# Two tokens per descriptor for the first blocks: a change to a windowed attention and highway kernel

## The chip, the cores and the metric

The kernel runs on one core of a Trainium2 chip. A core has five engines with a queue of instructions each: TensorE (PE, matrix products and transposes), VectorE (DVE), ScalarE (ACT), GpSimd (POOL) and SyncE (SP). They run side by side and wait for one another through semaphores. Sixteen DMA engines move data between main memory and the core's own memory; their work is issued by SP, ACT and POOL. The metric is the device time of one execution in microseconds, as a median of several runs. The time before is 115.41 us, the median of three runs from 115.22 to 116.79.

## What is computed

Four sequences (B) of 768 tokens, eight heads of 64 numbers each. Every query sees the four first keys of its sequence (the sinks) and the 128 keys up to its own position; then a highway layer runs over the 512 numbers of each token:

```python
scores = scale * q @ k.T                       # per batch and head
keep = (pos_k < 4) | ((rel >= 0) & (rel < 128))
a = softmax(where(keep, scores, -1e9))
x = (a @ v)                                    # heads side by side: 3072 x 512
H = maximum(x @ w_h, 0)
T = 1 / (1 + exp(-(x @ w_t + b_t)))
out = T * H + (1 - T) * x                      # float32, 3072 x 512
```

Inputs and output are float32 in main memory; the products run in fp16 with float32 sums.

## The kernel before

The 3072 tokens are cut into 24 blocks of 128, six to a batch; block n belongs to batch n // 6. All work is written as small steps, each for one block, and a single string `_STEPS` (lines 21 to 56) gives their order. The loop at lines 470 to 472 runs through it and emits the instructions of each step. An engine carries out its own instructions strictly in the order of this string, so the string is five queues in one. The planning is thus done beforehand, and nothing is reordered later.

The steps of one block, in the order of the data:

- `lq`, `lk` (`load`, line 140) bring q and k of a block, `[128 tokens, 8 heads, 64]`. For blocks 2 to 23 POOL issues them (line 150), and the DMA casts to fp16. For blocks 0 and 1 SP loads q and ACT loads k in float32 (line 143), and `cvq`, `cvk` (line 168) cast on DVE.
- `lv` (line 146) brings v of one block into `v_all`, for the blocks of batch 0. `lv0`, `lv1` (`load_v`, line 153) bring v of a whole later batch into `v_bat` (`vb` in the profile) in two parts of four heads, all six blocks at once. Every head's 64 columns have a column of ones behind them, so that the product with the weights gives the row sum too.
- `T` (line 258): sixteen transposes on PE of 64 tokens by two heads, out of both partition halves; `cT` (line 272) copies q and k transposed from PSUM to `qk` on ACT, in one instruction of 128x1024.
- `S0`, `S1` (line 304): scores of two head pairs each against the block and its predecessor; `E0`, `E1` (line 320): the exponential on ACT, 128x1024 (128x512 for the first block of a batch); `M0`, `M1` (line 329): the mask on DVE.
- `pks`, `sk`, `es`, `BA`: the sinks. `pks` (line 278) copies sink keys on POOL once per batch, and issues the load of the next batch's sink values; `sv` (line 174) spreads them on DVE. `BA` (line 344) also puts the bias row of the block before into its tile.
- `AV` (line 353): the product with v; `rec` and `x` (lines 375, 380) divide by the row sum on DVE.
- `X`, `cX` (or `cXd` on DVE), `Tt`, `u`, `H`, `d`, `g`, `ee`, `od`: the highway layer. PE transposes x (line 387) and multiplies by both weights (lines 407 and 422, with `lw_t` and `lw_h` loading them); ACT takes a tanh (`u`); DVE does `d`, `g`, `ee` and the last sum in `od` (line 447), whose output SP stores.

Constants: `first` (line 182) sets the ones, the mask and the identity and starts eight matmuls on a zero tile; `pm` and `pb` (lines 194, 202) shape masks on POOL; `K1` copies them; `load_bt` (line 216) loads the bias row twice, on SP, ahead of q; `K2` (line 220) clears the bias rows, sets rows of ones and casts the bias row twice on DVE; `K3` clears `ks_bd`, `K4` (line 233) sets the ones columns of `v_bat` and clears `vs_bd` and `es_t`; `K5` finishes the sink values of batch 0. `_FILL` (line 20) puts idle matmuls ahead of some steps on PE.

Buffers: eight for q and k each, two pairs of PSUM banks for `T` and the scores, one for `AV` and `X` together, two for `Tt`, `H` and `sk`.

Of the kernel before, what the change touches and what calls it, by code (L numbers as in the profile page):

```python
# [8 lines left out]
FP16 = mybir.dt.float16  # L9
# [12 lines left out]
    lk:0 lq:2 lsv:0 K4:0 pm:0 K1:0 cvk:0 lk:1 lbt:0 lq:0 cvq:0 T:0 cT:0 K3:0 S1:0 E1:0 S0:0 E0:0  # L22
    cvk:1 lq:1 cvq:1 T:1 K2:0 lq:3 lv:0 M1:0 cT:1 S1:1 E1:1 S0:1 M0:0 AV:0 lk:2 lk:3 rec:0 x:0 T:3
    E0:1 lv:1 T:2 M1:1 X:0 cT:2 cXd:0 M0:1 S0:2 AV:1 rec:1 x:1 cT:3 S1:3 lw_t:0 lk:4 pb:0 K5:0 pks:0
    E0:2 sv:6 E1:3 M1:3 M0:2 lq:4 S1:2 E1:2 sk:2 es:2 X:1 cX:1 Tt:0 u:0 T:4 cT:4 S0:3 lv:2 M1:2 E0:3
    lw_h:0 BA:2 AV:2 rec:2 x:2 M0:3 Tt:1 u:1 lq:5 g:1 lk:5 g:0 lv:3 X:2 cX:2 S1:4 H:0 d:0 E1:4 M1:4
    H:1 lq:7 T:5 S0:4 d:1 lk:7 ee:1 cT:5 E0:4 BA:3 AV:3 rec:3 lq:6 Tt:2 u:2 sk:4 es:4 x:3 od:1 X:3
    cX:3 S1:5 g:2 ee:0 M0:4 lv:4 E1:5 H:2 S0:5 d:2 E0:5 BA:4 AV:4 od:0 rec:4 lk:6 T:6 lv:5 ee:2 x:4
    cT:6 od:2 lv0:6 Tt:3 M0:5 u:3 X:4 lk:8 cX:4 T:7 cT:7 M1:5 S0:6 H:3 BA:5 AV:5 d:3 g:3 ee:3 lq:8
    E0:6 S1:6 E1:6 rec:5 S0:7 x:5 Tt:4 X:5 od:3 M1:6 E0:7 M0:7 u:4 g:4 T:8 S1:7 lv1:6 cX:5 E1:7 M0:6  # L30
    H:4 Tt:5 lk:9 d:4 lq:9 AV:6 M1:7 cT:8 u:5 ee:4 lk:10 S1:8 E1:8 rec:6 lq:10 x:6 pks:6 H:5 X:6
    od:4 d:5 S0:8 g:5 ee:5 T:9 cX:6 AV:7 rec:7 x:7 lk:11 Tt:6 E0:8 X:7 od:5 cT:9 S1:9 cXd:7 u:6 sk:8
    M0:8 lq:11 lk:13 g:6 E1:9 lk:12 es:8 lq:12 H:6 lq:13 T:10 cT:10 M1:8 d:6 ee:6 S0:9 E0:9 BA:8
    AV:8 rec:8 Tt:7 u:7 T:11 lk:14 cT:11 x:8 X:8 S1:10 od:6 cXd:8 H:7 M0:9 BA:9 E1:10 M1:9 S0:10 d:7
    AV:9 E0:10 rec:9 x:9 g:7 ee:7 M0:10 Tt:8 lq:14 u:8 T:12 X:9 od:7 g:8 cT:12 M1:10 lv0:12 cX:9
    sk:10 es:10 H:8 d:8 S1:11 E1:11 S0:11 E0:11 sv:12 BA:10 AV:10 rec:10 x:10 Tt:9 T:13 ee:8 u:9
    S0:12 E0:12 M1:11 X:10 lv1:12 M0:11 H:9 M0:12 S1:12 cX:10 BA:11 pks:12 lk:15 od:8 AV:11 rec:11
    cT:13 g:9 E1:12 T:14 cT:14 Tt:10 x:11 X:11 cX:11 d:9 ee:9 M1:12 S1:13 S0:13 H:10 od:9 u:10 g:10
    AV:12 rec:12 x:12 E0:13 Tt:11 lq:15 T:15 d:10 M0:13 E1:13 M1:13 lk:18 ee:10 u:11 g:11 X:12 S1:14
    H:11 d:11 cX:12 E1:14 cT:15 AV:13 od:10 S0:14 E0:14 Tt:12 sk:14 u:12 es:14 ee:11 S1:15 E1:15  # L40
    rec:13 lq:17 S0:15 x:13 X:13 od:11 lk:17 lk:16 M0:14 cX:13 M1:14 H:12 d:12 lq:20 T:17 g:12 BA:14
    AV:14 rec:14 x:14 E0:15 lq:16 T:16 M0:15 cT:17 lq:18 ee:12 Tt:13 X:14 lv0:18 M1:15 cT:16 H:13
    cX:14 S1:16 S0:16 u:13 d:13 od:12 E1:16 E0:16 lq:19 BA:15 lv1:18 g:13 AV:15 sk:16 rec:15 ee:13
    S0:17 es:16 E0:17 Tt:14 u:14 x:15 od:13 lk:19 lk:20 S1:17 M0:16 X:15 cX:15 E1:17 H:14 T:18 BA:16
    M1:16 M0:17 AV:16 d:14 Tt:15 cT:18 S0:18 T:19 pks:18 rec:16 g:14 u:15 x:16 X:16 cX:16 E0:18
    ee:14 od:14 H:15 M1:17 BA:17 M0:18 S1:18 g:15 lq:21 d:15 AV:17 rec:17 x:17 Tt:16 lk:21 cT:19
    S1:19 ee:15 E1:18 M1:18 T:20 X:17 cXd:17 u:16 g:16 H:16 od:15 AV:18 cT:20 E1:19 lq:22 rec:18
    x:18 S0:19 d:16 E0:19 M0:19 M1:19 Tt:17 u:17 S1:20 X:18 T:21 cX:18 H:17 cT:21 ee:16 lk:22 AV:19
    d:17 T:22 rec:19 E1:20 x:19 od:16 cT:22 g:17 sk:20 es:20 sv:18 S0:20 ee:17 M1:20 E0:20 M0:20
    X:19 Tt:18 u:18 lq:23 cX:19 od:17 H:18 d:18 S0:21 E0:21 S1:21 E1:21 BA:20 AV:20 rec:20 g:18  # L50
    lk:23 Tt:19 T:23 S1:22 u:19 x:20 M0:21 X:20 cX:20 ee:18 M1:21 cT:23 od:18 g:19 H:19 d:19 BA:21
    AV:21 E1:22 rec:21 S0:22 E0:22 Tt:20 ee:19 x:21 u:20 od:19 M0:22 M1:22 sk:22 S1:23 X:21 cX:21
    S0:23 H:20 es:22 BA:22 AV:22 g:20 d:20 rec:22 x:22 ee:20 E1:23 E0:23 M0:23 Tt:21 u:21 X:22 cX:22
    H:21 M1:23 BA:23 AV:23 d:21 g:21 rec:23 x:23 od:20 Tt:22 u:22 ee:21 g:22 od:21 X:23 cX:23 H:22
    d:22 ee:22 od:22 Tt:23 u:23 g:23 H:23 d:23 ee:23 od:23
# [4 lines left out]
def kernel(  # L60
# [48 lines left out]
    NV = NSC  # L109
# [3 lines left out]
    v_bat = [const.tile([P, VBW + 8], FP16, tag=f"vb{i}", name=f"vb{i}") for i in range(B - 1)]  # L113
# [15 lines left out]
    es_t = [const.tile([P, 2, P], FP16, tag=f"es{i}", name=f"es{i}") for i in range(2)]  # L129
    f32 = {(x, n): const.tile([P, H, D], FP32, tag=f"{x}f{n}", name=f"{x}f{n}")  # L130
           for x, ns in (("q", HWQ), ("k", HWK)) for n in ns}
    f16 = {(x, n): const.tile([P, H, D], FP16, tag=f"{x}h{n}", name=f"{x}h{n}") for x, n in f32}

    sd_of = {}

# [24 lines left out]
    def v_cols(n, h):  # L160
        b, c = divmod(n, NSC)
        if b == 0:
            return v_all[:, n, 65 * h:65 * h + _AVN]
        o = (h * NSC + c) * 65
        return v_bat[b - 1][:, o:o + _AVN]
# [342 lines left out]
```

## Time and profile before

| | value |
|---|---|
| median of three runs | 115.41 us (115.22 to 116.79) |
| the profiled execution | 116.29 us, its span 114.6 us |
| busy: PE, DVE, ACT, POOL | 102.0, 102.2, 91.1, 60.8 us |
| packets in all, under 512 B | 79540, 75426 |
| POOL's DMA queue | 71904 packets, 9.98 MB |
| landing after issue: f32 k, f32 q | 3.9, 5.8 us (medians) |
| landing: q, k on POOL; v by block; v by half batch | 7.3, 7.0; 7.0; 10.8 us |
| issue on POOL: q or k; v by block; half a batch of v | 0.91, 0.90, 1.45 us each |

The profile is of one execution. Its page has the busy time of the engines, the span in forty slices, the DMA queues, the chain of work that ended last, and groups of instructions by source line. Waits are listed as "who <- whom: us in total, times, longest". In the timeline a line gives start, duration, engine, source line, operation, output and inputs, and in brackets the idle time ahead of it with what ended it. Times are in us from the start of the span.

### The profile page before, as it was taken

The page shows a single profiled execution, that of the slowest core. Times are in us where ns is not written, and L with a number is a line of the kernel's source. Part 1 is how long each engine was busy: PE and PEld are TensorE (multiplying, and loading weights), DVE is VectorE, ACT ScalarE, POOL GpSimd, SP SyncE. Part 2 cuts the span into 40 slices and gives each one's busy share as a digit, 9 for nine tenths or more (in the row PEclk, how much of TensorE's full clock was granted, in tenths as well). Part 3 has the DMA queues.
Part 4 walks back from the last instruction along what each step waited for, and adds up shares of the span by engine and source line. Part 5 has one row for each costly group of instructions (what it writes and reads, how often), then busy time and mean ns, then how long its engine had stood idle before and what let it go on. Part 6 is the DMA issues. An engine that isn't in the chain of part 4 may idle for free.

```text
span 114.6 us, 3853 instructions
## 1 busy us (share of the span) xinstructions
PE 102.0 (89%) x1617; PEld 56.4 (49%) x1617; DVE 102.2 (89%) x236; ACT 91.1 (80%) x125; POOL 60.8 (53%) x79
## 2 busy tenths in 40 slices
PE   5956949999999899999999999999998999999910
PEld 2313535555555455556455655646554655644400
DVE  4649569699999999999999999999997999999990
ACT  3137699979999898989989999998898999982500
POOL 5999999796976199704999980003960000000000
PEclk9999999999999999999999999999999999999995
DMA  2999999999999999999999999991899222220332
GB/s 63 244 161 154 198 162 194 156 157 155 156 191 225 181 207 211 215 156 196 166 129 196 194 168 200 212 220 54 112 134 191 36 91 92 96 93 0 123 152 92
DMA packets 79540, 17.56 MB, mean 153 GB/s; under 512 B 75426, under 2 KB 76450, under 8 KB 79524
## 3 DMA queue, kind: packets, MB, share of 16 engines
q0 software_dynamic: 71904, 9.98, 132.0%
q1 hardware_dynamic: 5540, 6.82, 18.4%
q10 hardware_dynamic: 2080, 0.52, 2.0%
q8 instruction: 12, 0.20, 0.7%
q14 instruction: 4, 0.03, 0.1%
HBM read 21.01 MB, written 6.29 MB: 238 GB/s over the span
## 4 chain that ended last, share of the span: by engine, by line
DVE 31%; DMA 24%; PE 19%; POOL 15%; ACT 5%; issue 3%; POOLq 0%; ACTq 0%
DMA ksd<-in_k_dram 14%; DMA vb<-in_v_dram 10%; DVE e L335 8%; PE hps L426 6%; DVE otok L449 6%; DVE xh L382 5%; DVE dd L432 5%; POOL qsd L150 4%; PE av L368 3%; POOL ksd L150 3%; PE tps L414 3%; POOL v_all L146 3%; PE sps L316 3%; DVE gt L438 2%; DVE ee L444 2%
## 5 line engine op out<-in xcount | busy, mean ns | idle before, releaser
L324 ACT ACTIVATE e<-sps 128x1024 f16<-128x1024 f32 (+1 forms) x48 | 44.8, 961 | 2.2 <-PE sps L316 1.9
L274 ACT COPY qk<-tp 128x1024 f16<-128x1024 f16 x24 | 24.3, 1021 | 7.3 <-PE tp L268 7.3
L335 DVE TENSOR_TENSOR e<-e,mask 128x1024 f16<-128x1024 f16 (+1 forms) x48 | 29.2, 638 | 0.2
L426 PE MATMUL hps<-wh_sb,xT 128*128 128x512 f16 x96 | 24.7, 381 | 0.0
L414 PE MATMUL tps<-wt_sb,xT 128*128 128x512 f16 x96 | 24.7, 379 | 0.0
L150 POOL DMA_DIRECT2D ksd<-in_k_dram x22 | 19.9, 910 | 4.5 <-PE av L368 3.1
L150 POOL DMA_DIRECT2D qsd<-in_q_dram x22 | 20.1, 921 | 0.2
L419 ACT ACTIVATE u<-tps 128x512 f16<-128x512 f32 x24 | 14.5, 606 | 5.6 <-PE tps L414 5.4
L316 PE MATMUL sps<-qk 64*128 64x128 f16 x352 | 16.8, 217 | 1.7 <-ACT qk L274 1.7
L382 DVE TENSOR_TENSOR xh<-av,rec 128x512 f16<-128x512 f32 x24 | 16.5, 689 | 0.6
L432 DVE SCALAR_TENSOR_TENSOR dd<-hps,xh 128x512 f16<-128x512 f32 x24 | 16.4, 681 | 0.7 <-PE hps L426 0.7
L449 DVE TENSOR_TENSOR otok<-xh,ee 128x512 f32<-128x512 f16 x24 | 16.4, 683 | 0.1
L368 PEld LDWEIGHTS <-e 128*128 128x128 f16 x352 | 12.8, 97 | 5.5 <-DVE e L335 2.3
L316 PEld LDWEIGHTS <-qk 64*128 64x128 f16 x352 | 10.7, 94 | 8.6 <-issue 6.5
L404 ACT COPY xT<-xtp 128x512 f16<-128x512 f16 x20 | 11.8, 588 | 1.0 <-PE xtp L393 0.7
L368 PE MATMUL av<-vb,e 128*128 128x66 f16 x264 | 11.6, 194 | 0.6 <-DMA vb<-in_v_dram 0.4
L414 PEld LDWEIGHTS <-xT 128*128 128x128 f16 x96 | 8.2, 97 | 7.3
L426 PEld LDWEIGHTS <-xT 128*128 128x128 f16 x96 | 7.7, 98 | 8.0 <-issue 0.3
L285 POOL COPY ks<-qk 64x16 f16<-64x16 f16 x8 | 2.8, 349 | 16.2 <-ACT qk L274 16.0
L444 DVE TENSOR_TENSOR ee<-gt,dd 128x512 f16<-128x512 f16 x24 | 10.0, 417 | 0.3
L156 POOL DMA_DIRECT2D vb<-in_v_dram x6 | 8.7, 1449 | 1.2 <-DMA ksd<-in_k_dram 1.0
L438 DVE TENSOR_SCALAR gt<-u 128x512 f16<-128x512 f16 x24 | 8.6, 363 | 0.0
(66 smaller groups left out, 110.3 us busy)
## 6 DMA issues: line engine op xcount, KB each, us to landing
out_dram<-otok SPq DMA_DIRECT2D x24, 256.0 KB, 5.1
qsd<-in_q_dram POOLq DMA_DIRECT2D x22, 128.0 KB, 7.3
ksd<-in_k_dram POOLq DMA_DIRECT2D x22, 128.0 KB, 7.0
vb<-in_v_dram POOLq DMA_DIRECT2D x6, 384.0 KB, 10.8
v_all<-in_v_dram POOLq DMA_DIRECT2D x6, 128.0 KB, 7.0
kf<-in_k_dram ACTq DMA_DIRECT2D x2, 256.0 KB, 3.9
qf<-in_q_dram SPq DMA_DIRECT2D x2, 256.0 KB, 5.8
wt_sb<-in_moe_w_t_dram POOLq DMA_DIRECT2D x1, 512.0 KB, 6.9
```

The source lines that it names most:

```text
L150: nc.gpsimd.dma_start(out=sd, in_=dram(x, n))
L274: nc.scalar.copy(out=qk.rearrange("p j (a t) -> p a j t", a=2), in_=tp_of.pop(n)[:, :, 0:DM].rearrange("p a (j t) -> p a j t", t=64))
L316: nc.tensor.matmul(sps[:, hh, o:o + P], lhsT=kk[rows, hp, :], rhs=qT[rows, hp, :], start=True, stop=True)
L324: nc.scalar.activation(out=e.rearrange("p a b c d -> p a (b c d)"), in_=sps[:, :, 0:2 * np_ * P], func=AF.Exp, bias=_EXP_BIAS, scale=SCALE)
L335: nc.vector.tensor_tensor(out=ev, in0=ev, in1=m.unsqueeze(1).to_broadcast([P, 4, np_ * P]), op=ALU.mult)
L368: nc.tensor.matmul(av[:, g, 2 * hl + hh, 0:_AVN], lhsT=e[:, hh, hl, pc, :], rhs=v_cols(m, h), start=fresh, stop=False, skip_group_check=True)
L382: nc.vector.tensor_tensor(out=xh.rearrange("p (h d) -> p h d", d=D), in0=av_of.pop(n)[:, :, 0:D], in1=rec_of.pop(n).unsqueeze(2).to_broadc ...
L414: nc.tensor.matmul(t_of[n], lhsT=xT[:, kc, :], rhs=wt_sb[:, kc, :], start=False, stop=(kc == NOC - 1))
L419: nc.scalar.activation(out=uu, in_=t_of.pop(n), func=AF.Tanh, scale=0.5)
L426: nc.tensor.matmul(hps, lhsT=xT[:, kc, :], rhs=wh_sb[:, kc, :], start=(kc == 0), stop=(kc == NOC - 1))
L432: nc.vector.scalar_tensor_tensor(out=dd, in0=h_of.pop(n), scalar=0.0, in1=xh_of[n], op0=ALU.max, op1=ALU.subtract)
L449: nc.vector.tensor_tensor(out=otok, in0=xh_of.pop(n), in1=ee_of.pop(n), op=ALU.add)
```

## The change

Four things are changed together.

1. **q and k of blocks 0 and 1.** Partition p of half a holds the two tokens 2p and 2p+1 of heads 4a to 4a+3, so that each descriptor moves two neighbouring tokens of a head (512 bytes in place of 256). Each load is two DMAs, one per partition half. The cast on DVE sorts the two tokens apart, `T` still makes sixteen transposes, and `cT` puts the tokens back in order in two copies of 128x512.
2. **v of batch 1 by block.** `v_all` holds twelve blocks, `v_bat` two batches; `lv:6` to `lv:11` take the place of `lv0:6` and `lv1:6`.
3. **Constants split.** The two casts of the bias row leave `K2` (DVE) and become `K6` on ACT; the clearing of `vs_bd` and `es_t` leaves `K4` and becomes `K7`, still on DVE.
4. **The order.** `_STEPS` is new from the first to the last line.

```diff
 _STEPS = """
-    lk:0 lq:2 lsv:0 K4:0 pm:0 K1:0 cvk:0 lk:1 lbt:0 lq:0 cvq:0 T:0 cT:0 K3:0 S1:0 E1:0 S0:0 E0:0
-    cvk:1 lq:1 cvq:1 T:1 K2:0 lq:3 lv:0 M1:0 cT:1 S1:1 E1:1 S0:1 M0:0 AV:0 lk:2 lk:3 rec:0 x:0 T:3
-    E0:1 lv:1 T:2 M1:1 X:0 cT:2 cXd:0 M0:1 S0:2 AV:1 rec:1 x:1 cT:3 S1:3 lw_t:0 lk:4 pb:0 K5:0 pks:0
-    E0:2 sv:6 E1:3 M1:3 M0:2 lq:4 S1:2 E1:2 sk:2 es:2 X:1 cX:1 Tt:0 u:0 T:4 cT:4 S0:3 lv:2 M1:2 E0:3
-    lw_h:0 BA:2 AV:2 rec:2 x:2 M0:3 Tt:1 u:1 lq:5 g:1 lk:5 g:0 lv:3 X:2 cX:2 S1:4 H:0 d:0 E1:4 M1:4
...
+    lq:0 lk:0 lq:1 lk:1 lbt:0 pm:0 lk:3 K3:0 lq:3 K4:0 K2:0 cvk:0 K6:0 cvq:0 T:0 cT:0 cvk:1 S1:0
+    E1:0 S0:0 E0:0 cvq:1 T:1 K1:0 M0:0 cT:1 M1:0 K7:0 S1:1 E1:1 M1:1 lk:2 S0:1 E0:1 lsv:0 lv:0 AV:0
+    rec:0 x:0 lq:2 pb:0 T:2 cT:2 T:3 lw_t:0 K5:0 cT:3 pks:0 X:0 cXd:0 S0:2 E0:2 sv:6 sk:2 S1:2 E1:2
+    lv:1 S0:3 es:2 E0:3 M0:1 AV:1 M0:2 Tt:0 lw_h:0 u:0 rec:1 x:1 X:1 cX:1 lq:4 S1:3 E1:3 H:0 BA:2
+    lk:4 T:4 M1:2 g:0 M0:3 lv:2 d:0 ee:0 od:0 Tt:1 AV:2 cT:4 rec:2 S1:4 lk:6 u:1 g:1 S0:4 x:2 H:1
...
-    S0:17 es:16 E0:17 Tt:14 u:14 x:15 od:13 lk:19 lk:20 S1:17 M0:16 X:15 cX:15 E1:17 H:14 T:18 BA:16
-    M1:16 M0:17 AV:16 d:14 Tt:15 cT:18 S0:18 T:19 pks:18 rec:16 g:14 u:15 x:16 X:16 cX:16 E0:18
...
+    lq:19 lk:18 E0:16 Tt:14 u:14 sk:16 lv1:18 x:15 X:15 lv0:18 es:16 lq:20 cX:15 od:11 T:18 ee:13
+    cT:18 M0:16 H:14 S0:17 E0:17 M1:16 BA:16 od:13 g:14 pks:18 lq:21 d:14 lk:21 AV:16 S1:17 E1:17
...
-    H:21 M1:23 BA:23 AV:23 d:21 g:21 rec:23 x:23 od:20 Tt:22 u:22 ee:21 g:22 od:21 X:23 cX:23 H:22
-    d:22 ee:22 od:22 Tt:23 u:23 g:23 H:23 d:23 ee:23 od:23
+    M0:23 ee:20 E1:23 M1:23 Tt:21 u:21 X:22 cX:22 H:21 d:21 g:21 BA:23 AV:23 rec:23 x:23 ee:21 H:22
+    d:22 X:23 cX:23 Tt:22 od:20 u:22 od:21 Tt:23 u:23 g:22 ee:22 od:22 g:23 H:23 d:23 ee:23 od:23
 """
-    NV = NSC
+    NV = 2 * NSC
...
-    f32 = {(x, n): const.tile([P, H, D], FP32, tag=f"{x}f{n}", name=f"{x}f{n}")
+    f32 = {(x, n): const.tile([P, NHP, 2 * D], FP32, tag=f"{x}f{n}", name=f"{x}f{n}")
...
-    f16 = {(x, n): const.tile([P, H, D], FP16, tag=f"{x}h{n}", name=f"{x}h{n}") for x, n in f32}
+    f16 = {(x, n): const.tile([P, 2, NHP, D], FP16, tag=f"{x}h{n}", name=f"{x}h{n}") for x, n in f32}
     def load(x, n):
         if (x, n) in f32:
             eng = nc.sync if x == "q" else nc.scalar
-            eng.dma_start(out=f32[x, n], in_=dram(x, n))
+            b, c = divmod(n, NSC)
+            src = {"q": q, "k": k}[x][b, :, c * P:(c + 1) * P, :]
+            for a in range(2):
+                eng.dma_start(out=f32[x, n][64 * a:64 * a + 64],
+                              in_=src[NHP * a:NHP * a + NHP].rearrange("h (p t) d -> p h (t d)", t=2))
...
     def convert(x, n):
-        nc.vector.tensor_copy(out=f16[x, n], in_=f32[x, n])
+        nc.vector.tensor_copy(out=f16[x, n].rearrange("p t h d -> p h t d"),
+                              in_=f32[x, n].rearrange("p h (t d) -> p h t d", t=2))
...
         for r in (0, 64):
             nc.vector.memset(ones_row[r:r + 1, :], 1.0)
-            nc.vector.tensor_copy(out=bt16[r:r + 1, :], in_=bt32[r:r + 1, :])
+
+    def K6():
+        for r in (0, 64):
+            nc.scalar.copy(out=bt16[r:r + 1, :], in_=bt32[r:r + 1, :])
...
+    def K7():
         for i in range(2):
             nc.vector.memset(vs_bd[i], 0.0)
             nc.vector.memset(es_t[i], 0.0)
...
+        if ("q", n) in f32:
+            for i, sd in enumerate((qsd, ksd)):
+                for j in range(2):
+                    for t in range(2):
+                        for a in range(2):
+                            rows = slice(64 * a, 64 * a + 64)
+                            o = ((i * 2 + j) * 2 + t) * 64
+                            nc.tensor.transpose(tp[:, a, o:o + 64], sd[rows, t, 2 * j:2 * j + 2, :],
+                                                ident[rows, rows])
...
     def cT(n):
         qk = qkT_pool.tile([P, 2 * NHP, P], FP16, tag="qk", name="qk")
-        nc.scalar.copy(out=qk.rearrange("p j (a t) -> p a j t", a=2),
-                       in_=tp_of.pop(n)[:, :, 0:DM].rearrange("p a (j t) -> p a j t", t=64))
+        if ("q", n) in f32:
+            src = tp_of.pop(n)[:, :, 0:DM].rearrange("p a (i j t s) -> p a i j t s", i=2, j=2, t=2)
+            dst = qk.rearrange("p (i a j) (s t) -> p a i j t s", i=2, a=2, t=2)
+            for a in range(2):
+                nc.scalar.copy(out=dst[:, a], in_=src[:, a])
+        else:
+            nc.scalar.copy(out=qk.rearrange("p j (a t) -> p a j t", a=2),
+                           in_=tp_of.pop(n)[:, :, 0:DM].rearrange("p a (j t) -> p a j t", t=64))
```

`v_cols` and `load_v` follow the new sizes of `v_all` and `v_bat`, and `K6` and `K7` are added to the table of steps.

## The prediction

> **What bounds the kernel now.** I read the page first, then the waits, then the timeline of each engine. Parts 1 and 2 of the page give the busy shares and the span in forty slices of 2.9 us:
>
> ```profile
> PE 102.0 (89%) x1617; PEld 56.4 (49%) x1617; DVE 102.2 (89%) x236; ACT 91.1 (80%) x125; POOL 60.8 (53%) x79
> ...
> DVE  4649569699999999999999999999997999999990
> ACT  3137699979999898989989999998898999982500
> ```
>
> The DVE row is read from the left: mixed digits in the first nine slices (26 us), then a wall of nines up to the last slice. DVE is busy 102.2 of 114.6 us. Windows of the same trace put its 12.4 us of idle time at 2.7 us before 6 us, 1.6 us from 6 to 12, 1.1 from 12 to 14, 0.9 from 14 to 18, 1.0 from 20 to 25, and only 2.0 us in all of 25 to 110; 3.2 us lie behind its last instruction. So VectorE is the bound from 25 us on. A change can win in three places only: DVE work taken out, the idle time of the start, and the few late waits. The waits of DVE name them:
>
> ```profile
> DVE rec L377 <- PE av L368: 3.2, 5, 1.2
> DVE qh L168 <- DMA qf<-in_q_dram: 2.2, 2, 1.6
> DVE dd L432 <- PE hps L426: 0.7, 1, 0.7
> ```
>
> Four of the five waits for av lie at 13.04, 16.40, 21.29 and 39.44 us and take 1.17, 0.89, 0.82 and 0.16 us; the wait for hps is at 88.65. ScalarE's timeline shows what paces the start:
>
> ```profile
> 7.50 1.01 ACT L274 COPY qk<-tp 128x1024 f16<-128x1024 f16 x1 [4.33 <-PE tp L268]
> 8.90 1.09 ACT L324 ACTIVATE e<-sps 128x512 f16<-128x512 f32 x2 [0.38 <-PE sps L316]
> 10.30 1.01 ACT L274 COPY qk<-tp 128x1024 f16<-128x1024 f16 x1 [0.32 <-PE tp L268]
> 11.80 1.94 ACT L324 ACTIVATE e<-sps 128x1024 f16<-128x1024 f32 x2 [0.49 <-PE sps L316]
> 14.30 1.93 ACT L274 COPY qk<-tp 128x1024 f16<-128x1024 f16 x2 [0.56 <-PE tp L268]
> ```
>
> From its first copy at 7.50 ScalarE runs with gaps of half a microsecond, each copy of block 0 and 1 releasing scores, and the scores an exponential. The start of cT:0 is the term to follow.
>
> **The loads of blocks 0 and 1.** Now each moves 1024 runs of 256 B; afterwards 512 runs of 512 B, in two issues. The ACT queue (q10) carried 2080 packets in 2.0% of 16 engines' 114.6 us: 36.7 us, or 17.6 ns a packet. In the window of 60 to 90 us the output queue took 20.0% of 480 us for 1151 packets of 2 KB, 83 ns each. A straight line between the two gives about 27 ns for 512 B (my estimate). The four tiles then cost 2048 x 27 / 16 = 3.5 us against 4096 x 17.6 / 16 = 4.5: 1.0 us less. The last of them, q of block 1, lands at 1.94 + 6.5 = 8.45 now, that of block 0 at 6.57. With q0 and k0 first on both queues (data flows from 2.0 us at 209 to 253 GB/s) 524 KB are in at about 4.5, and cvq:0 (0.43) ends at 5.0. T:0 doesn't start then: PE's fill matmuls in front of it run from 4.65 to 6.15. T:0 goes from 7.05 to about 6.2 and could release cT:0 at 6.6, 0.9 us before today.
>
> The Trainium skill, page "DMA: Bandwidth & Descriptors", speaks on both sides. Its section Specifications gives 512 B as the smallest transfer at full rate, which agrees with the direction of the two rows above. Its section "Rules for kernel authors" says not to bother splitting a transfer over two partition halves, since both halves run on the same engines one behind the other; no run here shows that yet. By that rule the halves win nothing over one issue and only the run length counts; the sum above already takes nothing for the halves.
>
> **K6, the bias casts on ScalarE.** Two casts of 1x512 leave DVE (1.16 us) and go to ACT between cvk:0 and T:0, thus ahead of cT:0 in ACT's queue. The trace has no such row on ACT; 128x512 forms take 0.59 (copy) and 0.61 (tanh), so the pair costs between 0 and 1.2 us; I take 1.1. They wait for bt32, and its two DMAs, now first on SP at 0.81 and 1.22, are issued last, behind four issues of 0.41 to 0.72 us. The second is then issued between 3.0 and 4.3 and, with the 2.0 us that the quickest DMA of the trace takes to land, can be there at 5.0 at the earliest. On SP's queue the tiles land in the order of issue (6.57, 8.45), so I expect bt behind q1. Now the f32 tiles need 6.45 us from 2.0 on, 4.5 of their own and 1.9 shared with the POOL loads; afterwards 3.5 and, as the first POOL load moves behind the mask selects (1.7 to about 2.3), some 1.2 shared: 6.7. The ends are 5.0 and 8.45; I take 6.7, nearest to the row of q1 less the saved microsecond. K6 ends at 7.8 and cT:0 starts there, against 7.50. Queued behind K6 on ACT are cT:0, E1:0, E0:0, cT:1, and for cT:0 wait S1:0, pks:0 and with it POOL's next loads.
>
> **cT in two halves.** 128x512 copies take 0.59 each: 1.18 for 1.01, the strided write unknown; between -0.1 and +0.4 each, taken as +0.15, for two blocks +0.3. The same 16 transposes are issued in T. **Start: cT:0 from 7.8 to 8.95 instead of 8.51, and 0.15 more in block 1: +0.6** (bounds -0.65 and +2.4).
>
> **The DVE edits.** K4 loses one buffer's two memsets (0.16), v_all's two memsets double (0.09 more at most). K7 (1.3 us) moves from 2.6 us to behind M1:0. K2's casts now end at 11.08 and hold M0:0 back from 9.99 to 11.11; but DVE waits for av right after, so their going is worth nothing there: 13.04 is set by AV:0. The permuted casts of q and k write runs of 64 elements; 0.36 to 0.54 us now, at most doubled, beside idle DVE time. If that cover went, 0.4 us in block 0.
>
> **The order from 13 to 25 us.** Afterwards M1:1 can start at about 13.4 (E1:1's end plus the shift). DVE's queue then reads rec, x, K5, cXd, sv, M0:1, M0:2, rec, x, M1:2. Eleven instructions at their row times, less the 0.07 us by which neighbours overlap, are 6.0 us: M1:2 ends at 19.4 without a wait, if lv:1 (issued about 10.1, landing 5.7 to 9.0 later in the v_all row) is in for AV:1 at 17.2. Today M1:2 ends at 20.47 with one more mask (0.6) in it: 0.5 ahead. Then M0:3, g:0, d:0, ee:0 and od:0 (2.4 us) stand in front of rec:2, where today 0.82 us are idle; H:0 and Tt:1 ahead of AV:2 on PE take 2 us, so about half of that wait returns. I take **-0.6**, the ends being -1.9 (all idle time gone) and +0.8 (one more wait of the size of 0.82).
>
> **v of batch 1 by block.** POOL pays 6 x 0.90 for 2 x 1.45, +2.5 us. What hides it: POOL waits 16.0 us at pks. The six are issued one by one and AV:6 no longer needs both halves of vb, which now hold it at 39.1:
>
> ```profile
> PE av L368 <- DMA vb<-in_v_dram: 0.4, 1, 0.4
> POOL ks L285 <- ACT qk L274: 16.0, 2, 10.9
> PE tp L268 <- DMA ksd<-in_k_dram: 0.6, 1, 0.6
> ```
>
> DVE idles 0.16 us there: **-0.2** (0 to -0.2). If the cover goes, lv:6 comes late for AV:6; by issue times of 0.9 it goes out near 27 and lands near 35, some 3 us early.
>
> **T:21.** The third line above is at 87.35: k of block 21 is issued at 80.49, because POOL stood at pks:18 until cT:18 ended at 78.95. DVE idles 0.71 us at 88.65 for it. In the new order cT:18 stands ahead of E0:17 and E1:17 on ACT (two times 1.03), and PE has H:14, S0:17 and S1:17 more between T:18 and T:21. The load is early by more than the 0.6 it lacked; next late on PE is only its own work. **-0.6** (0 to -0.7).
>
> **Tail.** From x:23 on DVE has the same eleven instructions; now 0.26 us lie in a gap at 106.6 that od:20 and od:21 would fill: **-0.15** (+0.3 to -0.3).
>
> **Sum:** 0.6 - 0.6 - 0.2 - 0.6 - 0.15 = -0.95. The profiled execution took 116.29 (span 114.6 and 1.7 around it), 0.9 above the median of 115.41: 115.3 for such an execution, 114.5 as a median.
>
> **Rivals.**
> 1. *The bias row comes last and ScalarE stands in front of it.* For it: SP's two tiles landed in order, and 8.45 for q1 is measured while 512 B is an estimate. Against it: fewer packets. If bt lands at 8.45, K6 ends at 9.55 and cT:0 at 10.7: +2.35 for the start, -1.55 from the rest: 116.2, slower. It decides from a landing of 7.65 on (K6 to 8.75, cT:0 to 9.9). If AV:1 or AV:2 waits too (+0.8 for -0.6), 117.6. By the page's rule on halves the loads win least, and this is the case that it favours. Chance 0.24.
> 2. *The bias row is early*, since it is a few packets that needn't wait for all engines. At 5.0 K6 is over by 6.1, T:0 sets cT:0 at 6.6: start -0.65 + 0.15 and, the exponentials coming half a microsecond earlier, up to -1.5 in the second stage: 115.41 - 0.5 - 1.5 - 0.95 = 112.5. Chance 0.22.
> 3. *The order gives nothing*: waits move, DVE stays full after 25 us, and T:21's wait comes back at another block: 115.41 + 0.6 - 0.2 - 0.15 = 115.7, no change. Chance 0.14.
>
> The forecast has 0.40. The range 112.2 to 117.2 takes in rivals 2 and 1 and leaves out both worst ends (111.5 and 118.4). Two per cent, which is about what a measurement of this kernel can tell, is 113.1 and 117.7. Faster by more: rival 2 and a little of the forecast, 0.24; slower by more: the worse part of rival 1, 0.10; within: 0.66.
>
> **What would show it.** The first cast on ACT (1x512) starts near 6.7 and waits for DMA bt; T:0 near 6.2; the first copy of block 0 at 7.8 in two rows of 0.59. DVE has no wait of 0.9 for av between 14 and 18, none at 39 and none for hps near 88; its busy time is 1.2 us lower. The prediction is wrong if bt lands after 7.65 or before 5.5, if AV:1 waits for v_all, or if a wait of over half a microsecond appears on DVE behind 25 us.

## The result and the profile after

The changed kernel takes **120.86 us** (median of four runs, 120.29 to 121.43) against 115.67 for the kernel before in the same comparison (115.22 to 116.79): a ratio of **1.042, with an interval of 1.035 to 1.048**. It is slower; the forecast was 114.5, and the whole range ended at 117.2. An execution can be disturbed (the kernel before itself ran from 115.1 to 119.2 on the chips used below), and ratios are formed from the undisturbed ones alone, so that a ratio and two medians need not agree to the last half per cent.

The profiled execution took 121.43 us with a span of 119.7, 5.1 more than the 114.6 of before. Parts 1 and 2 of the page of the kernel after (busy time; then forty slices of 3.0 us):

```profile
PE 104.8 (88%) x1617; PEld 57.6 (48%) x1617; DVE 102.4 (86%) x232; ACT 92.7 (77%) x129; POOL 62.3 (52%) x83
...
DVE  5354065889999999999999999999999999999980
ACT  0007858999999788998898999999989999893500
...
PEclk9997555999999999999999999999999999999999
```

DVE is busy as long as before (102.4 for 102.2 us), although two casts have left it. Its wall of nines begins in the tenth slice (27 us) and has no gap up to the tail; before, it began in the ninth (23 us) and had a 7 at 86 to 89 us. ACT does nothing at all in the first three slices. And the clock granted to TensorE falls to half in slices 5 to 7, where the row of before has no low digit but the last:

```profile
PEclk9999999999999999999999999999999999999995
```

What ACT was waiting for stands in its timeline (start, duration, line, operation, idle time ahead of it and what ended it):

```profile
0.81 2.70 ACTq L146 DMA_DIRECT2D kf<-in_k_dram  x4
9.68 1.28 ACT L235 ACT_TABLE_LOAD   x1 [9.68 <-DMA bt<-in_moe_b_t_dram]
10.98 1.24 ACT L235 CAST bt<-bt 1x512 f16<-1x512 f32 x2
12.23 1.32 ACT L299 COPY qk<-tp 128x512 f16<-128x512 f16 x2
14.04 1.08 ACT L351 ACTIVATE e<-sps 128x512 f16<-128x512 f32 x2 [0.49 <-PE sps L343]
15.86 1.32 ACT L299 COPY qk<-tp 128x512 f16<-128x512 f16 x2 [0.73 <-PE tp L280]
```

The wait for the bias row ends at 9.68. Only then does ACT load its function table, then it casts the bias row twice, and cT:0 starts at 12.23 instead of 7.50. Before, the table load waited for nothing and was over by 3.2 us:

```profile
1.89 1.28 ACT L274 ACT_TABLE_LOAD   x1 [1.89 <-issue]
```

The transposes that cT:0 copies had been ready since 8.1.

The waits of DVE in the kernel after (who, for whom, us in total, times, longest):

```profile
DVE e L362 <- ACT e L351: 6.0, 3, 4.1
DVE kh L172 <- DMA kf<-in_k_dram: 3.2, 2, 1.7
DVE warm L188 <- PEq L517: 0.9, 1, 0.9
DVE rec L404 <- PE av L395: 0.7, 2, 0.4
```

The waits for av have shrunk from 3.2 to 0.7 us, and the one for hps is gone. In their place the first masks wait 6.0 us for the first exponentials.

**Two halves of the story.** Let the first reciprocal (rec:0) divide the span. It starts at 13.04 before and at 19.94 after: the start has lost 6.9 us. From rec:0 to the last reciprocal (rec:23) it was 92.0 us and is now 90.0: everything behind the start has won 2.0. The tail behind rec:23 is 9.7 for 9.55. 6.9 - 2.0 + 0.2 is the 5.1 us of the span. Windows from rec:0 to rec:23 show where the 2.0 come from (length, then busy time of PE, PEld, DVE, ACT, POOL). Before:

```profile
13.04:105.05 92.01, 88.24 (x1508) 50.85 (x1507) 88.16 (x188) 83.80 (x116) 49.12 (x57) 1.00 1.67 157
```

After:

```profile
19.94:109.97 90.03, 88.44 (x1508) 51.25 (x1507) 87.85 (x187) 83.12 (x116) 48.74 (x58) 1.00 1.68 153
```

DVE's idle time between the two marks goes from 3.85 us (92.01 - 88.16) to 2.18: 1.67 us less. The rest is DVE's own durations, 0.3 us.

**The 6.9 us of the start** add up from single rows: cT:0 starts 4.73 later, is 0.31 longer (two copies of 0.66 for one of 1.01), and from its end to rec:0 it takes 6.39 us instead of 4.53, 1.86 more. This last part has the low clock in it. The windows of after that hold it (columns as above, the eighth number is the clock):

```profile
9.00:11.00 2.00, 0.00 (x0) 0.00 (x0) 1.30 (x6) 1.30 (x2) 0.00 (x0) 0.81 3.14 141
11.00:14.00 3.00, 0.40 (x8) 0.34 (x8) 0.06 (x1) 2.52 (x4) 0.33 (x3) 0.50 1.60 193
14.00:18.00 4.00, 3.50 (x33) 1.41 (x30) 2.03 (x6) 2.53 (x5) 4.00 (x7) 0.50 0.80 54
18.00:21.00 3.00, 2.97 (x37) 1.54 (x35) 1.71 (x6) 2.44 (x3) 3.00 (x4) 0.58 1.17 162
```

PE runs out of work at 8.8 and waits for the copy cT:0 until 13.6. A mean of 0.81 in the window of 9 to 11 puts the drop near 10.2, and 0.58 in that of 18 to 21 the return near 20.5. In between eight score products take 0.61 us where they took 0.40.

### The profile page after: what moved, and what is told of

Same layout as the page of the kernel before. It is cut to its first block, busy times and chain, and to the rows that moved or that the text cites. A ratio compares the mean times of both kernels' runs of the same rounds, so it can differ in the third digit from the quotient of the medians.

```text
span 119.7 us, 3869 instructions
## 1 busy us (share of the span) xinstructions
PE 104.8 (88%) x1617; PEld 57.6 (48%) x1617; DVE 102.4 (86%) x232; ACT 92.7 (77%) x129; POOL 62.3 (52%) x83
## 4 chain that ended last, share of the span: by engine, by line
PE 57%; DVE 27%; DMA 7%; ACT 5%; issue 1%; ACTq 0%
PE hps L453 13%; PE tps L441 11%; PE sps L343 9%; PE av L395 8%; DVE e L362 5%; DMA bt<-in_moe_b_t_dram 5%; DVE otok L476 5%; DVE dd L459 5%; DVE xh L409 5%; PE tp L289 4%; DVE ee L471 3%; DVE gt L465 3%; DMA kf<-in_k_dram 3%; PE sk L323 2%; PE xtp L420 2%; PE sps L258 2%
## 5 line engine op out<-in xcount | busy, mean ns | idle before, releaser
L301 ACT COPY qk<-tp 128x1024 f16<-128x1024 f16 x22 | 22.1, 1020 | 0.8 <-PE tp L289 0.7
L343 PE MATMUL sps<-qk 64*128 64x128 f16 x352 | 17.5, 224 | 4.8 <-ACT qk L299 4.8
L409 DVE TENSOR_TENSOR xh<-av,rec 128x512 f16<-128x512 f32 x24 | 16.5, 688 | 0.6
L476 DVE TENSOR_TENSOR otok<-xh,ee 128x512 f32<-128x512 f16 x24 | 16.3, 685 | 0.2
L459 DVE SCALAR_TENSOR_TENSOR dd<-hps,xh 128x512 f16<-128x512 f32 x24 | 16.3, 680 | 0.0
L312 POOL COPY ks<-qk 64x16 f16<-64x16 f16 x8 | 2.3, 285 | 22.7 <-ACT qk L301 17.5
L150 POOL DMA_DIRECT2D v_all<-in_v_dram x12 | 10.9, 908 | 1.7 <-DMA wh_sb<-in_moe_w_h_dram 1.3
L235 ACT ACT_TABLE_LOAD x1 | 1.3, 1283 | 9.7 <-DMA bt<-in_moe_b_t_dram 9.7
```

Source lines behind the costliest of these rows:

```text
L301: nc.scalar.copy(out=qk.rearrange("p j (a t) -> p a j t", a=2), in_=tp_of.pop(n)[:, :, 0:DM].rearrange("p a (j t) -> p a j t", t=64))
L343: nc.tensor.matmul(sps[:, hh, o:o + P], lhsT=kk[rows, hp, :], rhs=qT[rows, hp, :], start=True, stop=True)
L409: nc.vector.tensor_tensor(out=xh.rearrange("p (h d) -> p h d", d=D), in0=av_of.pop(n)[:, :, 0:D], in1=rec_of.pop(n).unsqueeze(2).to_broadc ...
L459: nc.vector.scalar_tensor_tensor(out=dd, in0=h_of.pop(n), scalar=0.0, in1=xh_of[n], op0=ALU.max, op1=ALU.subtract)
L476: nc.vector.tensor_tensor(out=otok, in0=xh_of.pop(n), in1=ee_of.pop(n), op=ALU.add)
```

## The experiments

The theory from these profiles was: *the bias row comes last on SP's queue, and everything on ACT stands behind it*. Rivals were that the new loads themselves are late, that the halved clock is the price, that the table load behind the wait is, and that the new order is worse. Each kernel below is the one named, with one edit. cT:0 and rec:0 are start times from the profile of the run; the ratio is to the kernel before on the same chip, with its interval of 95%.

**1. Bias row first, all else as after (e1_bt_first).**

```diff
-    lq:0 lk:0 lq:1 lk:1 lbt:0 pm:0 lk:3 ...
+    lbt:0 lq:0 lk:0 lq:1 lk:1 pm:0 lk:3 ...
```

> The changed kernel with the bias row's load first on SP instead of last. Theory A (ScalarE's queue stands behind the bias row: it landed at 9.68 us, then came the table load of 1.28, the casts of 1.24 and only then cT:0 at 12.23): cT:0 starts at the end of T:0, near 8.3, TensorE's clock doesn't drop at 10 us, and the time falls by 4.0 to 4.8 us to about 116.4. Theory C (the new order or the loads are what is slow): cT:0 starts early all the same, but the time falls by less than 2 us, to 119 or more.

Measured: 117.49 us, ratio 1.011 (1.006 to 1.016). Some 3% of the 4.2% are gone, so the place of the bias row on the queue carries most of the loss. But the kernel is still not faster than before, and against the expectation the clock fell here too (from 9.6 to 16.4 us). ACT's timeline in this run:

```profile
3.88 1.28 ACT L239 ACT_TABLE_LOAD   x1 [3.88 <-issue]
5.18 1.25 ACT L239 CAST bt<-bt 1x512 f16<-1x512 f32 x2
7.74 1.32 ACT L303 COPY qk<-tp 128x512 f16<-128x512 f16 x2 [1.32 <-PE tp L284]
...
12.71 1.32 ACT L303 COPY qk<-tp 128x512 f16<-128x512 f16 x2 [2.18 <-PE tp L284]
```

cT:0 is back where it was (7.74), cT:1 isn't (12.71 for 10.30): q of block 1 is cast at 11.53 only, and DVE waits 2.3 us for it. With the bias row last (after) the same cast ran at 9.96, and with the old loads and the row first (5, below) at 8.21: in these profiles q is late with the new loads, and later still with the row's two issues ahead of it.

**2. More idle matmuls while PE waits (e2_fill).**

```diff
-_FILL = {'T:0': 4, 'S1:0': 3, ...
+_FILL = {'T:0': 4, 'S1:0': 25, ...
```

> The changed kernel with 25 idle matmuls ahead of S1:0 instead of 3, so that TensorE works from 8.0 to about 13.4 us, where it stood idle. Theory B (the halved clock from 10 to 21 us is a cost of its own): granted clock 1.0 throughout, S1:0 still at 13.6, and 1.0 to 2.0 us less: about 119.3. Theory A alone (only the late start counts, ScalarE paces the stretch anyway): within 0.4 us of the changed kernel, 120.5 to 121.

Measured: 121.02 us, ratio 1.032 (1.025 to 1.039). Inconclusive. In its profile the clock held until about 16.3 and then fell all the same, and the bias row, issued 0.7 us later, landed at 10.67, a microsecond later than in the profile of after. From the end of cT:0 to rec:0 it took 5.7 us for 6.4. The interval overlaps that of after.

**3. The table load ahead of the wait (e3_table).** An 8-element copy on ACT, of a tile that DVE has cleared, is put behind the two k loads; it has no part in the output.

```diff
-    lq:0 lk:0 lq:1 lk:1 lbt:0 ...
+    lq:0 lk:0 lq:1 lk:1 tb:0 lbt:0 ...
+        "tb": lambda n: nc.scalar.copy(out=tb_b, in_=tb_a),
```

> The changed kernel with a copy of 8 elements on ScalarE behind its loads of k, so that the table load comes there and not behind the wait for the bias row. Theory A: the table load is done by 6 us, the casts start at 9.7, cT:0 at 10.95 instead of 12.23, and the time falls by 1.3 us, and a little more for a shorter time at the halved clock: 119.2. If the late start is caught up later by idle time of VectorE: less than 0.4 us.

Measured: 119.94 us, ratio 1.023 (1.018 to 1.029), thus 1.8% below after. ACT in this run:

```profile
3.55 1.28 ACT L494 ACT_TABLE_LOAD   x1 [3.55 <-issue]
```

The table is now loaded at 3.55, and the casts start at 10.69 without it. That this is the landing of the bias row is inferred: the profile lists the wait under a mask instruction of DVE that ended just then, with which the casts have nothing to do. So the table load did stand on the path. It is 1.28 us long, 1.1% of the time; the 1.8% measured are more than that, within the intervals. The profile doesn't show the whole of it at the start: with the row a microsecond later, cT:0 is only 0.3 us earlier than in after and rec:0 0.35, and 1.15 us of its shorter span lie between rec:0 and rec:23, in shorter DVE instructions.

**4. The new loads alone (e4_loads).** The kernel before, with the loads, casts, `T` and `cT` of the change and its own order, constants and v.

> The kernel before with the new loads, casts, T and cT of blocks 0 and 1 alone; order, bias casts and v as before. Theory A, with the loads as measured in the changed kernel (an issue of a half takes 0.64 to 0.86 us against 0.41 to 0.72 for a whole tile, a 512-byte packet 35 ns against 17.6 for 256): no gain, cT:0 later by 0.3 to 1.0 and each cT by 0.3, 116.0 to 117.0. As I predicted the loads (27 ns a packet): cT:0 half a microsecond earlier, 115.0 to 115.6.

Measured: 118.52 us, ratio 1.012 (1.006 to 1.018). cT:0 at 8.54 and cT:1 at 12.17, against 7.50 and 10.30. The loads alone lose; the clock was at half from 7.5 to 14.3, and how much of the loss that makes isn't separated.

**5. All but the new loads, bias row first (e5_bt_first_old_loads).** After, with `lbt:0` first as in 1 and `load`, `convert`, `T`, `cT` of before.

> The changed kernel with the bias row's load first on SP and the old loads, casts, T and cT for blocks 0 and 1: what is left of the change is the new order, v of batch 1 by block and the casts on ScalarE. Theory A (the bias row's place and the loads make up the whole loss; with the bias row first 1.1% of it is left, and the loads alone cost 1.15%): cT:0 starts by 7.6 us, the clock holds, ratio to the kernel before 0.990 to 1.003. Theory C (the new order costs something of its own): ratio above 1.006.

Measured: 114.25 us, ratio **0.978 (0.967 to 0.989): faster than before**. ACT in this run:

```profile
2.19 1.28 ACT L234 ACT_TABLE_LOAD   x1 [2.19 <-DMA bt<-in_moe_b_t_dram]
3.48 1.25 ACT L234 CAST bt<-bt 1x512 f16<-1x512 f32 x2
8.11 1.01 ACT L283 COPY qk<-tp 128x1024 f16<-128x1024 f16 x1 [3.37 <-PE tp L277]
```

The wait for the bias row is still on the table load, but the row is there at 2.19, 1.4 us after its issue at 0.81, and all of it is over 3.4 us before cT:0 can start. The gain was more than expected, although cT:0 starts at 8.11 and not by 7.6 and the clock fell (from 9.8 to 13.3). What is left of the change, the order with v by block and the split constants, gains: 88.7 us from rec:0 to rec:23 where it was 92.0. Of these 3.3 us, 1.7 are less idle time of DVE, as forecast; the other 1.6 are shorter instructions on DVE, which nobody forecast (1.2 of them in the `g` steps, of which more in the last section).

**6. All but the new loads, bias row still last (e6_old_loads).** After, with the four functions of before; the bias row now stands behind two issues on SP instead of four.

> The changed kernel with the old loads, casts, T and cT alone; the bias row stays last on SP, behind two issues instead of four. Theory A1 (the bias row lands behind whatever stands on SP's queue; q of block 1 landed at 8.45 in the kernel before): it lands at 8.0 to 9.0, the table load and the casts end 2.5 us later, cT:0 starts near 11.0, ratio 1.025 to 1.035. Theory A2 (it was the four slow issues that made the bias row late; issued at 2.0 it lands by 5.5): cT:0 before 8.2, ratio below 1.01.

Measured: 117.80 us, ratio 1.013 (1.008 to 1.018); cT:0 at 9.96, between what the theories gave. The difference to 5, on the same chip, is the place of the bias row alone: 3.5%. The row was issued at 1.92 here and is waited for until 7.38:

```profile
7.38 1.28 ACT L230 ACT_TABLE_LOAD   x1 [7.38 <-DMA bt<-in_moe_b_t_dram]
```

That is 5.5 us after issue behind two loads; in after it is 5.7 us behind four (3.93 to 9.68), in 5 it is 1.4 behind none. The time is not made of so much per issue ahead: in these profiles the 2 KB row lands about when the loads ahead of it do.

**7 and 8. What in the loads is late: the two issues, or the longer runs?** One kernel splits the load of before over partition halves and keeps its runs of 256 B (e7_halves); the other has runs of 512 B in one issue over 64 partitions (e8_one_issue). Both start from the kernel before.

```diff
-            eng.dma_start(out=f32[x, n], in_=dram(x, n))
+            for a in range(2):
+                eng.dma_start(out=f32[x, n][64 * a:64 * a + 64], in_=dram(x, n)[64 * a:64 * a + 64])
```

```diff
-            eng.dma_start(out=f32[x, n], in_=dram(x, n))
+            eng.dma_start(out=f32[x, n], in_=src.rearrange("h (p t) d -> p h (t d)", t=2))
```

In the second, the first diff being e7's, all eight heads lie on partitions 0 to 63, `T` reads both head halves from there, and `convert` and `cT` are those of the change.

> The kernel before with the f32 loads of blocks 0 and 1 issued as two partition halves each, runs of 256 bytes as before. If the second issue is what makes the new loads slow (0.64 to 0.86 us for each half): q of block 0 lands after 7.0, cT:0 starts at 8.0 to 8.7, the clock drops at about 8 us, ratio 1.006 to 1.015, as with the new loads alone. If it is the runs of 512 bytes (35 ns a packet, no gain per byte): landings as in the kernel before (6.6 and 8.5), ratio 1.000 to 1.004. By the rule of the Trainium skill (page DMA: Bandwidth & Descriptors, section Rules for kernel authors) that halves go one behind the other on the same engines, the data itself takes as long as before, and only the issues are added.

> The kernel before with runs of 512 bytes in a single issue: two tokens of all eight heads on 64 partitions, transposes out of those 64, cT in two copies. The casts take 64 partitions x 1024 elements, about 0.9 us each instead of 0.45. If the second issue is the slow part: a tile's issue takes 0.4 to 0.7 us and q of block 0 lands by 6.2, earlier than before. If 512-byte packets are no faster per byte: it lands at 6.6 or later. The time of the whole is not the point here, since casts and cT are longer: 115.7 to 118.

Measured: e7 120.73 us (118.88 to 121.61), ratio 1.027 (1.012 to 1.041), more than expected; e8 118.10 us, ratio 1.016 (1.005 to 1.026). Both lose, each in its own way. The loads of q in the two kernels (issue on SP, durations in ns least/median/most, first and last start; then the time to landing). Kernel e7:

```profile
L144 SPq DMA_DIRECT2D qf<-in_q_dram x4: 596/632/694, 1.5 to 4.3; - x4
...
DMA to landing us min/median/max: 4.8/6.0/6.6
```

Kernel e8:

```profile
L145 SPq DMA_DIRECT2D qf<-in_q_dram x2: 625/652/679, 1.5 to 2.2; - x2
...
DMA to landing us min/median/max: 5.0/6.8/8.5
```

Half a tile takes as long to issue as a whole one (0.60 to 0.69 us; the two whole tiles of before took 0.41 and 0.72), so two halves cost twice the issue time, and the last is issued at 4.3 instead of 1.9; q of block 1 is cast at 12.55 instead of 8.50. In one issue of 512-byte runs this is avoided, but then the landing itself takes 8.5 us for q of block 1 where it took 6.5. Fewer packets were no cheaper there: queue q10 of e8 carried 1056 packets in 2.4% of 16 engines' span, 42 ns each, against 17.6 for half the bytes before. (In e8 the casts on 64 partitions are longer too, 0.69 to 1.00 us, and `cT` has two halves; both are part of its loss. Whether the longer runs or the 64 partitions make its landing late isn't separated.)

**9. The clock, with the good version (e9_clock).** Kernel 5, with idle matmuls that leave PE no gap ahead of T:0.

```diff
-_FILL = {'T:0': 4, 'S1:0': 3, 'T:1': 1, ...
+_FILL = {'T:0': 9, 'S1:0': 4, 'S0:0': 1, 'T:1': 1, ...
```

> The kernel with the bias row first and the old loads, with more idle matmuls: nine ahead of T:0 (four before), four ahead of S1:0 (three), one ahead of S0:0, so that TensorE has no gap of 1.1 us ahead of T:0. Theory B (the halved clock is a cost of its own): the clock stays at 1.0 where it fell to 0.5 from 9.9 to 13.3 us, S1:1 and S0:1 end about 0.8 us earlier, ratio to the kernel before 0.966 to 0.974. Theory A alone (ScalarE and the landings pace this stretch): 0.976 to 0.982, as without them.

Measured: 113.98 us, ratio 0.986 (0.977 to 0.994). The window of 9 to 11 us shows the clock held (5 has 0.71 there, and 0.62 from 11 to 14):

```profile
9.00:11.00 2.00, 1.71 (x28) 0.82 (x28) 0.54 (x4) 1.35 (x3) 1.66 (x4) 1.00 2.74 150
```

From the end of cT:0 to rec:0 it is 4.96 us for 5.79 in 5: 0.8 us on the path of the start. In the total it can't be told from 5; the intervals overlap, and the ratio lies above what either theory gave.

**10. v of batch 1 back in two parts (e10_v_halves).** Kernel 5, with `v_all` and `v_bat` of before, and the two parts `lv0:6` and `lv1:6` in place of `lv:6` to `lv:11`; `lv:5` changes places with the first part, since block 5 needs it sooner.

```diff
-    ... lv:7 T:7 BA:4 AV:4 E0:5 lv:5 ...   lv:6 lq:11   lv:8 ... lv:11
+    ... lv:5 T:7 BA:4 AV:4 E0:5 lv0:6 ...  lv1:6 lq:11
```

> The kernel with the bias row first and the old loads, with v of batch 1 in two parts of four heads again. My prediction gave v by block 0.2 us: ratio 0.976 to 0.984. If POOL's shorter issue (2 x 1.45 for 6 x 0.90 us) counts more: below 0.976; if AV:6 comes to wait for the second half: 0.985 to 0.995, with a wait of AV for vb of over half a microsecond near 35 us.

Measured: 117.02 us, ratio 1.004 (0.998 to 1.011), where kernel 9 on the same chip has 0.986: 1.9% of 115.4, or 2.2 us, and more than any of the three cases expected. AV:6 waits for the second part of v, and DVE for AV:6. The lines of PE and of DVE:

```profile
40.38 0.28 PE L377 MATMUL av<-vb,e 128*128 128x66 f16 x4 [2.37 <-DMA vb<-in_v_dram]
```

```profile
40.70 0.21 DVE L386 RECIPROCAL rec<-av 128x8 f32<-128x8 f32 x1 [2.35 <-PE av L377]
```

(The profiled execution took 117.85 us, its quickest 115.86; the place of the wait is from the profile, the price from the ratio.) Without v by block the new order is worth nothing that can be measured.

**11. The bias casts on DVE again (e11_casts_dve).** Kernel 5, with K6 on DVE.

```diff
-            nc.scalar.copy(out=bt16[r:r + 1, :], ...
+            nc.vector.tensor_copy(out=bt16[r:r + 1, :], ...
```

> The kernel with the bias row first and the old loads, with the two casts of the bias row on VectorE at the same place in the order (behind the cast of k of block 0, where VectorE waits for q). If their move to ScalarE is worth nothing with the bias row there, as I predicted for the place of the casts: ratio 0.974 to 0.983. If ScalarE was relieved or VectorE is short of time there: 0.984 to 0.990.

Measured: 113.94 us, ratio 0.984 (0.976 to 0.992), as kernel 9 on the same chip. Moving the two casts off DVE neither gains nor costs once the row is there in time. (Kernel 9 has its fills as a second difference; 14 below differs from 9 by the casts alone and has 0.985 for 0.986, on another chip.)

**12. The casts later on ACT, the rest as after (e12_casts_later).** The bias row stays last on SP; only K6 moves behind E0:1.

```diff
-    ... cvk:0 K6:0 cvq:0 T:0 cT:0 ... S0:1 E0:1 lsv:0
+    ... cvk:0 cvq:0 T:0 cT:0 ...      S0:1 E0:1 K6:0 lsv:0
```

> The changed kernel with its new loads and the bias row last on SP, the two casts on ScalarE moved behind E0:1. Theory A (it is the place in ScalarE's queue that costs, not the late bias row itself): the table load is over by 5.5 us, cT:0 starts at T:0's end near 8, ratio 1.008 to 1.022, as with the bias row first (1.011) and up to 1.2 us for casts in a busy stretch. If it isn't the queue: 1.03 or more.

Measured: 117.65 us, ratio 1.017 (1.009 to 1.025). ACT in this run:

```profile
3.82 1.28 ACT L303 ACT_TABLE_LOAD   x1 [3.82 <-issue]
8.44 1.32 ACT L303 COPY qk<-tp 128x512 f16<-128x512 f16 x2 [3.34 <-PE tp L284]
```

With the same loads and the bias row as late on the queue, cT:0 starts at 8.44 and not at 12.23; the casts run at 16.64 without a wait. So a late row costs nothing by itself; the place of its casts in ACT's queue did. The ratio is close to that of 1, and what remains above kernel 5 is put down to the loads, with a clock at half from 9.7 to 16.5.

**13. v by block alone, in the old order (e13_v_alone).** The kernel before, with twelve blocks in `v_all`, `lv:6` and `lv:7` at the places of the two parts and `lv:8` to `lv:11` behind the q loads of blocks 9 to 12.

> The kernel before with v of batch 1 by block alone, its loads put where the halves stood and behind q of blocks 9 to 12. If the late stall is worth what it shows in the kernel before (0.16 us of VectorE at 39.4 us): ratio 0.995 to 1.003. If v by block is worth two per cent by itself, as in the new order: 0.975 to 0.985. In the first case the wait for vb is only as short as it is because the old order reaches AV:6 late, and two parts of the change are worth something only together.

Measured: 117.65 us as a median of four, its quickest 115.48 where the kernel before had 115.11 on the same chip; no ratio could be formed. No wait for v is left at AV:6, and the stretch from rec:0 to rec:23 is 91.8 us with 4.1 of DVE idle, against 92.0 with 3.9: its profile shows no gain. What v by block is worth in the old order stays open.

**14 and 15. Casts on DVE with and without the fills (e14_casts_dve_clock, e15_casts_dve_again).** Kernel 11 with the fills of 9, and kernel 11 once more.

> New order, v by block, bias row first, old loads, casts of the bias row on VectorE, and the added idle matmuls ahead of T:0, S1:0 and S0:0. Theory B: the clock stays at 1.0, the path from cT:0 to rec:0 is 0.5 to 0.9 us shorter than without them, and the time is 0.3 to 0.8 us below that of the kernel without them. Theory A alone: no difference between the two.

> The same kernel without the added idle matmuls: the clock falls to half for some 3 us behind 9 us. Ratio to the kernel before 0.978 to 0.988 by either theory; it is the other half of the comparison.

Measured: 113.78 us, ratio 0.985 (0.980 to 0.991), and 113.84 us, 0.984 (0.979 to 0.990). The same. But in the profile of the second the clock held too (mean 0.988 over the span), so the pair doesn't price the clock. In both it is 4.95 us from the end of cT:0 to rec:0, as in 9. Kernels 11 and 15 do price it, for they are one program: in the profile of 11 the clock was at half from 9.8 to 13.2, and this way took 5.66 us, 0.7 more.

**The parts together.** Order, v by block and split constants with the bias row first: -2.2% in kernel 5, -1.5 to -1.6% in 9, 11, 14 and 15. The new loads on top: +3.3% against 5 (1), 2.6% against the other four; 12, where the bias row is out of the way in another manner, says +3.2% against those four. The bias row last instead of first: +3.0% with the new loads (after against 1), +3.5% with the old ones (6 against 5). So two parts of about 3% each stand against one of about 2%. In the old order the loads took 1.2% (4); why they cost more in the new one was not settled. In the profile of every kernel with the new loads the clock was at half for 6.8 us or longer at the start (3.4 in 2), so what a late landing costs and what the clock costs are one sum here. The best versions, 5, 9, 11, 14 and 15, take 113.8 to 114.3 us, 1.5 to 2.2% less than the kernel before.

## Why the prediction was wrong

**What bounds the kernel: right.** From rec:0 on DVE is the bound in both kernels (idle 3.85 of 92 and 2.18 of 90 us), and a lost start is not made up behind it.

**The loads: this step failed first.** It took 27 ns for a packet of 512 B, on a straight line between two rows, and from it that the tiles land a microsecond earlier. The sum counted packets and left out the issues. In the changed kernel each half takes 0.62 to 0.86 us to issue. The loads of q in after:

```profile
L146 SPq DMA_DIRECT2D qf<-in_q_dram x4: 624/669/860, 0.8 to 3.2; - x4
...
DMA to landing us min/median/max: 5.2/5.7/6.7
```

And in the kernel before:

```profile
L143 SPq DMA_DIRECT2D qf<-in_q_dram x2: 413/566/718, 1.5 to 1.9; - x2
...
DMA to landing us min/median/max: 5.1/5.8/6.5
```

For q nothing has changed from issue to landing (medians 5.7 and 5.8), though each issue brings half as much. The last issue is 1.3 us later (3.2 for 1.9), and q of block 1 is cast at 9.96 instead of 8.5: later by just about that. For k the last issue is 1.6 us later (2.9 for 1.3) and the way to landing longer too (median 4.9 for 3.9, longest 6.2 for 4.7): by these figures k of block 0 landed at 5.8 for 4.0, and k of block 1 at 9.1 for 6.0. T:0 started at 7.66, not at 6.2. Of this, 0.8 us are longer casts of block 0, 0.90 and 0.76; the writing in runs of 64 isn't the reason, since in kernel 1 the same casts took 0.43 each. The packet itself had no one price: 27.5 ns in e4, 35 in after, 42 in e8 (q10's share of the span over its packets), for 17.6 with half the bytes. At its best that is a fifth less per byte, at its worst a fifth more.

The prediction weighed two sections of the Trainium skill, page "DMA: Bandwidth & Descriptors". Section Specifications has 512 B as the smallest transfer at full rate; here runs of 512 B came in no sooner than runs of 256 B (q of block 0 is cast at 6.58 in e8 and at 6.57 in the kernel before). Its "Rules for kernel authors" say not to split a transfer over partition halves; e7 agrees (1.027), and shows as a reason what the section doesn't name, the second issue.

**K6: right in its mechanism, far too small in size.** The prediction put the bias row "behind q1", and it did land close to q of block 1 (9.68, cast of q1 at 9.96). What was wrong was when that is: 6.7 was taken and 8.45 named as the latest, since q1 was thought to come earlier than today, never later. That is 3.0 us. The second miss, 1.3 us, was in no term: the table load stands ahead of the first activation on ACT, and by moving casts that wait for a DMA to the head of ACT's queue the change put the wait ahead of the table load as well. In before the load ran at 1.89 beside the DMAs, and had no part in the sum. The casts took 1.24 for 1.1. 3.0 + 1.3 + 0.1 is the way from the predicted 7.8 to 12.23.

The Trainium skill, page "ScalarE: Activation LUTs", section "What ACT_TABLE_LOAD costs", gives 1283 ns for the load itself; the 1.28 us in all the timelines above agree. No run here shows the drain that it adds for a switch from one set to another.

**Rival 1** (bias row last, ScalarE in front) named this cause; kernels 1, 6 and 12 show it. The landing from which it was to decide, 7.65, was too late: in kernel 6 the row landed at 7.38, and its place still cost 3.5%, since the table load comes on top. Its price was wrong by 4.7 us (116.2 for 120.86): it took 8.45 for the landing, left the table load out, and gave the gain of the other steps in full against a delay of 2.35 that was really 6.9 at rec:0.

**What follows cT:0.** The start was taken to shift as a whole, with 0.15 us more for block 1's copy. Instead the way from cT:0 to rec:0 grew by 1.86 us. By single profiles: 0.43 are in the new order itself (4.96 in e9 with the old loads and a full clock, against 4.53 before), 0.83 in a clock halved for 3.4 us (5.79 in 5 against 4.96 in 9), 0.40 more where it is halved for nearly the whole way (6.19 in 6, still with the old loads), and the last 0.20 (6.39 in after) come with the new loads, whose cT:1 is 0.31 longer. So the halved clock, which was a rival, is some 1.2 of the 6.9 us of the start. The prediction read the clock row as full and didn't ask what keeps it so.

**cT in two halves:** 0.31 more per block, in the bounds (0.15 taken).

**Order, v by block, T:21: right.** Predicted -0.6, -0.2 and -0.6, together -1.4. Measured: 1.67 us less idle time on DVE from rec:0 to rec:23, of it 0.83 up to rec:7 (predicted 0.8 for order and v) and 0.84 behind it (0.6 for T:21). It isn't a gift of the late start, which gives the loads more time: kernel 5, with rec:0 at 14.91, has 1.72 less. No wait stands at AV:6 or T:21. **The tail** won nothing (0.15 predicted): from rec:23 to the end of the last DVE instruction it is 6.44 us in both. One size in it was misread: v by block was priced by the 0.16 us that DVE waited in the old order, but in the new one, which needs v sooner, the two parts would have cost 2.2 us (10). Whether it is a gain by itself is open (13); it is what the new order rests on.

**The DVE edits: right** in that they are worth nothing (11). But DVE's busy time was to fall by 1.2 us and rose by 0.2: the casts of q and k took 2.5 us for 1.8, and the masks, `g` and K5 took 0.2 longer each.

## What to carry to other kernels

An instruction that waits for a DMA must not be placed ahead of urgent work on an in-order engine on the strength of an estimated landing: take it to land when the loads ahead of it on its queue have landed, and look whether a one-time cost of the engine, such as the table load, will be queued behind the same wait. A DMA in two halves costs two issues, and here the last half landed later by about as much as it was issued later. When a change of many parts fails, separate them: here one part gained about 2% and two lost about 3% each, and without those two the kernel is faster than the kernel before.

## What the runs showed of the hardware that was not expected

- The table load takes over the wait of the first activation behind it: with the bias casts first in ACT's queue it started at 9.68, 7.38 and 2.19 us, each time on the landing of the bias row (after, 6, 5); with a copy of an idle tile first (3) it ran at 3.55.
- The 2 KB bias row landed 1.4 us after issue at the head of SP's queue and 5.5 to 6.0 us behind the loads of q, with two or four of them ahead (6, after, 2).
- The granted clock was low for once, twice or three times 3.41 us. The thirteen low stretches that end within a trace lasted 3.4 us (2, 5, 8, 10, 11), 6.8 (1, 4, 6, 7, 12, 13) or 10.2 (after, 3; in after from 10.26 to 20.50). In the 3.41 us ahead of each of these falls PE was busy for 0.5 to 1.9 us; in the last 3.41 us ahead of each return for 3.1 or more, and in a low stretch that went on for 2.9 at most. So the gap just ahead of it doesn't make a fall: in 5 PE had no gap over 0.6 us between 7.66 and the fall at 9.84, but had been busy for only 1.7 of the last 3.41 us. The Trainium skill, page "TensorE: Matmul & The Clock Gate", Part 1, names a window of about 3.4 us that runs on its own, which agrees with these lengths; it puts the fall after an idle window, and here the windows ahead of a fall were not idle.
- DVE's times for one and the same instruction vary between executions and within one: the 24 `g` steps of after have a median of 0.286 us and reach 0.978, and sum to 8.8 us in after, 7.5 in kernel 5 and 8.6 before. These 1.3 us are the difference between after and 5 from rec:0 to rec:23 (90.0 and 88.7 us). In the seventeen traces every `g` over 0.32 us (86 of the 398 that the timelines list singly) ran while POOL was issuing a DMA, and of the 233 with no such issue beside them none did. Another 79 ran beside an issue and stayed short. What in the issue stretches a `g` no run tells.
